# Order of the output products, of the output evictions and of one convolution eviction in a fused convolution, gate and projection kernel

## The chip, the cores and the metric

The kernel runs on one core of a Trainium2 chip. A core has a matrix engine (TensorE, PE in the profile; its weight loads are PEld), three engines for element-wise work (VectorE or DVE, ScalarE or ACT, GpSimd or POOL), a queue that only issues transfers here (SyncE or SP), and 16 DMA engines. Each engine works through its own instructions in the order in which they were written, and waits at an instruction until the others have reached what it needs. The metric is the device time of one execution in microseconds.

## The reference

The reference has two stages over x of 8 sequences, 4224 tokens and 192 channels, all in fp32.

```
w    = softmax(weight, axis=-1) # 8 heads x 7
y[s] = sum_k w[h, k] * x[s - 6 + k]  # per head of 24 channels
pre  = sum_k conv_w[k] * y[s - 4 + k]  # 5 taps per channel
gate = 1 / (1 + exp(-pre))
out  = (gate * (y @ w_val)) @ w_out # two 192 x 192 products
```

So each token takes a 7-tap convolution, a 5-tap gate with a sigmoid, a product with `w_val`, a multiplication by the gate, and a product with `w_out`.

## The kernel before, in words

The 192 channels lie on partitions as 128 plus 64. The token stream is cut in two streams, so that chunk 0 of a tile holds the first 128 channels of both streams side by side (128 x 2 x m), and chunk 1 the remaining 64 channels of one stream in partitions 0 to 63 and of the other in 64 to 127 (128 x m). A *block* is m tokens of each stream. There are 37 blocks, 0 to 36 (`N`, `LAST` = 36): two of 288, six of 432, 27 of 482, one of 500 and one of 244.

Per block the work is this.

- The 7-tap convolution is made on the matrix engine from overlapping windows of x, with the softmaxed taps as a band matrix (`conv_unit`, L303). A unit takes up to 7 windows of 8 small matmuls each (four 64-row pieces, each of two instructions) into two PSUM banks `pc`, and ScalarE copies each bank into a buffer `e` (the *evictions*, L330). From there DMAs scatter the rows into the tiles `x1` and `x2` (`scatter`, L359), and new windows are loaded (L165); both are issued by SP. The units of a group of blocks are made about two groups ahead. Blocks 5 to 28 take two units each, of 14, 13 and 13 windows in turn; block 29 takes two, blocks 30 and 31 one, later blocks none.
- The gate's taps: ScalarE makes the first tap into a PSUM tile (`gate_open`, L393: `pa` for chunk 0, `pb` for chunk 1), VectorE adds the four others (`gate_taps`, L400), ScalarE takes the sigmoid (`gate_close`, L413, which writes `g`). Each of `pa` and `pb` has one buffer, so a gate is opened only after the one before it was closed.
- The *value* product v = y @ w_val and the *output* product o of the block before it. Each has a third of its columns for chunk 1 (`v_2`, `o_2`: `diagonal` L456 and `columns` L490, plain fp32) and two thirds for chunk 0 of the two streams (`v_0`, `v_1`, `o_0`, `o_1`), which are made with operands split into a high and a low fp32r part: `rows` (L479, from chunk 1) and `main` (L466, from chunk 0), three products each.
- The high parts are casts on ScalarE (`xh`, `ph`, L421 for chunk 0 and L429 for chunk 1), the low parts subtractions on POOL (`xl`, `pl`, L422 and L430). `ph` and `pl` are those of the gated values, on which the output product works.
- VectorE multiplies the value product by the gate (`gated`, L508: g <- v, g), ScalarE copies the output product to `ot` (`project`, L524), and SP sends it out (L529).

All of this is written out by hand, engine by engine; nothing reorders it. The v, o and pc banks share one pool of five PSUM banks, `ps`, given out in turn. A block with two units takes ten, so each tile of a block gets the same bank every time: v_2 and o_1 the first, o_2 and the first unit's first pc the second, v_0 and its second pc the third, v_1 and the second unit's first pc the fourth, o_0 and the second unit's second pc the fifth. A matmul that writes a bank first waits until its last reader has finished.

From block 4 (`HEAD`) on the loop at the end of the kernel sets the order. In letters, A is a tap of chunk 0's gate and B one of chunk 1's. The two closings of a block are: first that of chunk 1 (after taps B A B A), later that of chunk 0 (after taps A B A B).

Of the kernel before, what the change touches and what calls it, by code (L numbers as in the profile page):

```python
# [33 lines left out]
NJS = [2, 3, 3, 3] + [5] * 9 + [3]  # L34
# [71 lines left out]
def kernel(  # L106
# [193 lines left out]
                units.append((g, q, ws[i : i + UNIT[n]]))  # L300
    first_unit = [next(i for i, u in enumerate(units) if u[0] == g) for g in range(NG)] + [len(units)]

    def conv_unit(u):  # L303
        g, q, ws = units[u]
        n = NJS[g]
        if u == first_unit[g]:
# [19 lines left out]
        a = ws[0][0] * n + ws[0][1]  # L326
        w = len(ws)
        ev = e[:, : 4 * n * WIN].rearrange("p (w r t) -> p w r t", r=2, t=HW)
        for r in range(2):
            nc.scalar.copy(ev[:, a : a + w, r, :], pc[r][:M, : w * HW].rearrange("p (w t) -> p w t", t=HW))  # L330
        done = [hi for hi, j in ws if j == n - 1]
        for hi in done:
            h = QUADS[q][hi]
# [71 lines left out]
    def gate_close(n, i):  # L405
        if n >= N:
            return
        m = STEPS[n][2]
        if i == 0:
            dst = g1s[n] = gp.tile([128, 2, MB], F32, tag="g1", name=f"g1_{n}")[:, :, :m]  # L410
        else:
            dst = g2s[n] = gp.tile([128, MB], F32, tag="g2", name=f"g2_{n}")[:, :m]
        nc.scalar.activation(dst, accs.pop((n, i)), AF.Sigmoid)  # L413
# [122 lines left out]
        at.append(at[-1] + m)  # L536
    done = [0]

    def conv(k):
        for _ in range(k):  # L540
            if done[0] < len(units):
                conv_unit(done[0])
                done[0] += 1

    todo = [0] * (N + 1)
# [69 lines left out]
    gate_taps(HEAD, 1)  # L615
    for i in range(2):
        gate_close(HEAD, i)
    for i in range(2):
        gate_open(HEAD + 1, i)

# [15 lines left out]
    def close():  # L636
        for n, i in pending:
            gate_close(n, i)
# [6 lines left out]
    for n in range(HEAD, N + 1):  # L645
        diagonal(n)
        taps({HEAD: "", HEAD + 1: "BBABA"}.get(n, "BABA"))
        close()
        if n <= LAST:
            split_gated1(n - 1)  # L650
        reopen()
        split(n + 1)
        columns("v", n)
        gated(n, 2)
        columns("o", n - 1)
        project(n - 1, 2)
        split_gated2(n)
        taps("AABAA" if n == HEAD else "ABAB")
        close()
        reopen()  # L660
        rows("v", n)
        rows("o", n - 1)
        main("v", n, 0)
        gated(n, 0)
        main("v", n, 1)
        gated(n, 1)
        if n == LAST:
            split_gated1(n)
        main("o", n - 1, 0)
        project(n - 1, 0)  # L670
        main("o", n - 1, 1)
        project(n - 1, 1)
        conv(todo[n])


# [75 lines left out]
```

## Time and profile before

| | |
|---|---|
| time before, median of 3 | 366.2 us (364.02, 366.20, 366.21) |
| the profiled execution | 368.63 us, its span 366.8 us |
| granted matrix clock, mean over the span | 0.98 (0.93 and 0.90 up to 80 us, then 1.00 up to 345 us) |
| time from a closing of chunk 0's gate to the next, blocks of 482 with two units | 9.21 to 9.26 us (one of 11.52, one of 9.96) |
| the same, blocks without units | 8.72 and 8.73 us |

The profiled execution is taken by the hardware profiler, and is 0.7% longer than the median. In the rows, the first number is the start in us from the start of the span, the second the length in us. Starts that lie closer together than the lengths are pipelined: what an instruction occupies of its engine is the distance to the next one's start. A bracket at the end of a row says how long the engine was idle before it, and what ended this.

### The profile page before, as it was taken

What the parts mean: (1) busy time and instruction counts of PE and PEld (TensorE: products, weight loads), DVE (VectorE), ACT (ScalarE), POOL (GpSimd) and SP (SyncE); (2) the same over time, 40 slices, a digit from 0 to 9 for tenths busy, and PEclk for the clock granted to TensorE, in tenths of its full rate; (3) what the DMA queues carried; (4) which work ended last, traced back from release to release, by engine and by line L of the source; (5) the groups of instructions that cost most, each with busy time, mean ns of one, the idle gap of its engine ahead of it and who ended that gap; (6) DMA issues with size and microseconds to landing.
All of it is one profiled execution on the core that took longest, in us unless ns stands there. A gap on an engine that the chain in (4) does not pass through costs nothing.

```text
span 366.8 us, 13015 instructions
## 1 busy us (share of the span) xinstructions
PE 340.6 (93%) x5316; PEld 220.7 (60%) x5316; DVE 326.2 (89%) x439; ACT 306.4 (84%) x538; POOL 266.8 (73%) x209
## 2 busy tenths in 40 slices
PE   8887889799988999999999999999999999999995
PEld 8766456566655666665666666566666666554453
DVE  4898498989997999999999999899999999999970
ACT  7588588799886889889889889889889888888773
POOL 1959534677777777777777777777777777888883
PEclk9899699899999999999999999999999999999999
DMA  8899779898995998998998798898799796432233
GB/s 278 241 230 264 226 220 287 211 264 269 210 291 163 213 281 266 206 283 269 206 289 267 203 287 266 202 281 272 183 288 283 188 270 201 143 117 83 81 158 132
DMA packets 38948, 83.20 MB, mean 227 GB/s; under 512 B 4936, under 2 KB 17008, under 8 KB 38888
## 3 DMA queue, kind: packets, MB, share of 16 engines
q1 hardware_dynamic: 37440, 80.64, 74.6%
q0 software_dynamic: 896, 1.27, 1.5%
q8 instruction: 42, 0.69, 0.8%
q10 hardware_dynamic: 552, 0.46, 0.4%
q14 instruction: 18, 0.15, 0.2%
HBM read 30.06 MB, written 26.00 MB: 153 GB/s over the span
## 4 chain that ended last, share of the span: by engine, by line
PE 32%; DVE 30%; ACT 19%; DMA 9%; issue 6%; SPq 3%; DVEq 0%; POOL 0%; ACTq 0%
DVE pa L400 19%; PE pc L319 9%; PE v L490 7%; ACT pa L393 7%; ACT g L413 7%; DMA x<-xw 7%; DVE pb L400 7%; PE o L456 5%; DVE g L508 5%; ACT ot L524 4%; PE v L456 3%; PE v L466 2%; PE o L466 2%; DMA x<-e 2%; SPq L359 1%
## 5 line engine op out<-in xcount | busy, mean ns | idle before, releaser
L400 DVE SCALAR_TENSOR_TENSOR pa<-x,cwt,pa 128x964 f32<-128x964 f32 (+4 forms) x148 | 173.3, 1171 | 0.8 <-ACT pa L393 0.4
L422 POOL TENSOR_TENSOR pl<-g,ph 128x964 fp32r<-128x964 f32 (+4 forms) x37 | 80.0, 2161 | 75.6 <-ACT ph L421 70.1
L400 DVE SCALAR_TENSOR_TENSOR pb<-x,cwt,pb 128x482 f32<-128x482 f32 (+4 forms) x148 | 102.9, 695 | 0.6
L508 DVE TENSOR_TENSOR g<-v,g 128x482 f32<-128x482 f32 (+4 forms) x111 | 66.6, 630 | 25.8 <-PE v L490 21.0
L319 PE MATMUL pc<-band,x 64*64 64x58 f32 (+1 forms) x3776 | 75.3, 222 | 13.8 <-ACT ot L524 7.4
L319 PEld LDWEIGHTS pc<-band,x 64*56 64x56 f32 (+1 forms) x3776 | 66.3, 134 | 28.5 <-ACT ot L524 11.0
L422 POOL TENSOR_TENSOR xl<-x,xh 128x964 fp32r<-128x964 f32 (+4 forms) x37 | 73.4, 1984 | 3.3 <-ACT xh L421 3.3
L330 ACT COPY e<-pc 120x348 f32<-120x348 f32 (+2 forms) x148 | 59.3, 485 | 4.0 <-PE pc L319 3.9
L524 ACT COPY ot<-o 128x482 f32<-128x482 f32 (+4 forms) x111 | 57.2, 547 | 5.3 <-PE o L466 2.9
L413 ACT ACTIVATE g<-pa 128x964 f32<-128x964 f32 (+4 forms) x37 | 34.8, 940 | 30.8 <-DVE pa L400 30.8
L430 POOL TENSOR_TENSOR xl<-x,xh 128x482 fp32r<-128x482 f32 (+4 forms) x37 | 42.0, 1135 | 6.4 <-ACT xh L429 3.8
L430 POOL TENSOR_TENSOR pl<-g,ph 128x482 fp32r<-128x482 f32 (+4 forms) x37 | 43.2, 1167 | 1.5 <-ACT ph L429 1.5
L393 ACT ACTIVATE pa<-x,cwt 128x964 f32<-128x964 f32 (+4 forms) x37 | 38.1, 1030 | 1.9 <-DMA x<-e 0.7
L490 PE MATMUL v<-x,wvf 128*64 128x482 f32 (+4 forms) x148 | 37.3, 583 | 2.3 <-issue 2.3
L456 PE MATMUL o<-g,wof 64*64 64x482 f32 (+4 forms) x148 | 37.8, 572 | 0.2 <-issue 0.2
L421 ACT CAST ph<-g 128x964 fp32r<-128x964 f32 (+4 forms) x37 | 36.3, 980 | 1.8 <-POOL pl L430 1.8
L456 PE MATMUL v<-x,wvf 64*64 64x482 f32 (+4 forms) x148 | 36.5, 561 | 0.0
L421 ACT CAST xh<-x 128x964 fp32r<-128x964 f32 (+4 forms) x37 | 36.2, 979 | 0.0
L490 PE MATMUL o<-g,wof 128*64 128x482 f32 (+4 forms) x148 | 35.0, 550 | 0.0
L466 PE MATMUL v<-xh,wvh 128*128 128x482 f32 (+4 forms) x74 | 31.7, 429 | 0.0
L466 PE MATMUL o<-pl,woh 128*128 128x482 f32 (+4 forms) x74 | 27.5, 371 | 1.0 <-POOL pl L422 1.0
L466 PE MATMUL v<-xh,wvl 128*128 128x482 f32 (+4 forms) x74 | 27.8, 375 | 0.0
(68 smaller groups left out, 481.3 us busy)
## 6 DMA issues: line engine op xcount, KB each, us to landing
x<-xw SPq DMA_DIRECT2D x72, 300.0 KB
out<-ot SPq DMA_DIRECT2D x27, 723.0 KB
x<-e SPq DMA_DIRECT2D x45, 271.9 KB
x<-xw SPq DMA_DIRECT2D x16, 360.0 KB
x<-e SPq DMA_DIRECT2D x36, 135.9 KB
out<-ot SPq DMA_DIRECT2D x6, 648.0 KB
x<-e SPq DMA_DIRECT2D x20, 163.1 KB
x<-e SPq DMA_DIRECT2D x18, 90.6 KB
```

The lines of the kernel that those rows point to most:

```text
L319: nc.tensor.matmul(pc[r][c0:c1, k * HW : (k + 1) * HW], lhsT=xtiles[i][p, c + c0 : c + c1], rhs=band[p, 4 * q + hi, :], start=True, stop=True,
L393: nc.scalar.mul(acc, views(n, 0)[i], cwt[:, i, 0:1])
L400: nc.vector.scalar_tensor_tensor(out=acc, in0=views(n, k)[i], scalar=cwt[:, i, k : k + 1], in1=acc, op0=ALU.mult, op1=ALU.add,)
L413: nc.scalar.activation(dst, accs.pop((n, i)), AF.Sigmoid)
L421: nc.scalar.copy(h, x)
L422: nc.gpsimd.tensor_tensor(out=l, in0=x, in1=h.bitcast(F32), op=ALU.subtract)
L430: nc.gpsimd.tensor_tensor(out=l, in0=x, in1=h.bitcast(F32), op=ALU.subtract)
L456: nc.tensor.matmul(dst, lhsT=w22, rhs=x[HALVES[r]], start=True, stop=False)
L466: nc.tensor.matmul(acc, lhsT=a[:, r], rhs=b[:, q], start=(fresh and i == 0), stop=(not fresh and i == 2))
L490: nc.tensor.matmul(acc[HALVES[q if what == "v" else 1 - q]], lhsT=w.f[:, W12 : W12 + 64], rhs=x[:, q], start=False, stop=True)
L508: nc.vector.tensor_tensor(out=v, in0=banks.pop(("v", n, q)), in1=v, op=ALU.mult)
L524: nc.scalar.copy(ots[n][:, q * m : (q + 1) * m], banks.pop(("o", n, q)))
```

## The change

From block 4 on, five things stand in another order. No instruction is added or taken away, and the order on VectorE, POOL and SP is the same as before.

1. In blocks 4 to 35 the output product's `rows` and `main` go ahead of the value product's `main`, `rows` of o also ahead of `rows` of v. Since banks are given out in turn, the banks move too: o_0 takes the third bank, o_1 the fourth, v_0 the fifth and v_1 the first, which is that of v_2 of the same block.
2. With them `project` moves: ScalarE copies o_0 and o_1 to `ot` ahead of the second closing (chunk 0's gate), and not behind the opening that follows it.
3. The cast `ph` of the block before (`split_gated1`) goes ahead of the first closing (chunk 1's gate), and not behind it.
4. The second eviction of a block's last unit, and the scatters and loads that stand behind it, are held back until the first closing of the next block has been issued (`hold`, `held`, `release`).
5. In block 4 the cast of block 3 goes ahead of the two openings of the gates of block 5; blocks 36 and 37 keep the old order of the products.

```
-        for r in range(2):
+        def evict(r):
             nc.scalar.copy(ev[:, a : a + w, r, :], pc[r][:M, : w * HW]...)
+        evict(0)
+        if hold:
+            held.append(lambda: (evict(1), send_rows(g, q, ws, e)))
+        else:
+            evict(1)
+            send_rows(g, q, ws, e)
...
     for i in range(2):
         gate_close(HEAD, i)
+    split_gated1(HEAD - 1)
     for i in range(2):
         gate_open(HEAD + 1, i)
...
         diagonal(n)
         taps({HEAD: "", HEAD + 1: "BBABA"}.get(n, "BABA"))
+        if HEAD < n <= LAST:
+            split_gated1(n - 1)
         close()
-        if n <= LAST:
-            split_gated1(n - 1)
+        release()
         reopen()
...
+        def outputs():
+            for q in range(2):
+                main("o", n - 1, q)
+                project(n - 1, q)
+
+        if n < LAST:
+            rows("o", n - 1)
+            rows("v", n)
+            outputs()
+        else:
+            rows("v", n)
+            rows("o", n - 1)
         close()
         reopen()
-        rows("v", n)
-        rows("o", n - 1)
-        main("v", n, 0)
-        gated(n, 0)
-        main("v", n, 1)
-        gated(n, 1)
+        for q in range(2):
+            main("v", n, q)
+            gated(n, q)
         if n == LAST:
             split_gated1(n)
-        main("o", n - 1, 0)
-        project(n - 1, 0)
-        main("o", n - 1, 1)
-        project(n - 1, 1)
-        conv(todo[n])
+        if n >= LAST:
+            outputs()
+        conv(todo[n], True)
```

ScalarE before, from the closing of chunk 0's gate of block 12 (in the loop's block 11) to that of block 13; the first number in a name is the block, or the unit for pc:

```order
L413 ACTIVATE g1_12_2271<-pa_12_2126 128x2x482
L393 ACTIVATE pa_13_2273<-x1_5_1406,cwt_155 128x2x482
L524 COPY ot_10_2261<-o_10_0_2283 128x482
L524 COPY ot_10_2261<-o_10_1_2284 128x482
L330 COPY e_7_0_2310<-pc_34_0_2311 120x7x58
L330 COPY e_7_0_2310<-pc_34_1_2312 120x7x58
L330 COPY e_7_0_2310<-pc_35_0_2347 120x7x58
L330 COPY e_7_0_2310<-pc_35_1_2348 120x7x58
L413 ACTIVATE g2_12_2393<-pb_12_2246 128x482
L421 CAST ph_11_2395<-g1_11_2124 128x2x482
L393 ACTIVATE pb_13_2399<-x2_5_1407,cwt_155 128x482
L421 CAST xh_13_2405<-x1_5_1406 128x2x482
```

ScalarE after, at the same place, from the copies of o_10 on:

```order
L542 COPY ot_10_2261<-o_10_0_2271 128x482
L542 COPY ot_10_2261<-o_10_1_2272 128x482
L431 ACTIVATE g1_12_2296<-pa_12_2151 128x2x482
L411 ACTIVATE pa_13_2298<-x1_5_1406,cwt_155 128x2x482
L331 COPY e_7_0_2310<-pc_34_0_2311 120x7x58
L331 COPY e_7_0_2310<-pc_34_1_2312 120x7x58
L331 COPY e_7_0_2310<-pc_35_0_2347 120x7x58
L439 CAST ph_11_2388<-g1_11_2149 128x2x482
L431 ACTIVATE g2_12_2392<-pb_12_2246 128x482
L331 COPY e_7_0_2310<-pc_35_1_2348 120x7x58
L411 ACTIVATE pb_13_2399<-x2_5_1407,cwt_155 128x482
L439 CAST xh_13_2405<-x1_5_1406 128x2x482
```

The two copies to ot moved over the closing and the opening, the cast ph moved over one closing and one eviction, and that eviction moved behind the closing.

The matrix engine before, `rows` of block 12's values and of block 11's outputs, with what each waits for:

```order
L479 MATMUL v_12_0_2428<-xh2_12_2248,wvh_157 128x482 [waits Activation_49,Pool_49]
L479 MATMUL v_12_1_2429<-xh2_12_2248,wvh_157 128x482 [waits Activation_49]
L479 MATMUL v_12_0_2428<-xh2_12_2248,wvl_158 128x482
L479 MATMUL v_12_1_2429<-xh2_12_2248,wvl_158 128x482
L479 MATMUL v_12_0_2428<-xl2_12_2249,wvh_157 128x482 [waits Pool_49]
L479 MATMUL v_12_1_2429<-xl2_12_2249,wvh_157 128x482
L479 MATMUL o_11_0_2436<-ph2_11_2263,woh_161 128x482 [waits Activation_49]
L479 MATMUL o_11_1_2437<-ph2_11_2263,woh_161 128x482 [waits DVE_49]
```

The matrix engine after, at the same place:

```order
L497 MATMUL o_11_0_2424<-ph2_11_2263,woh_161 128x482 [waits Activation_49]
L497 MATMUL o_11_1_2425<-ph2_11_2263,woh_161 128x482 [waits Activation_49]
L497 MATMUL o_11_0_2424<-ph2_11_2263,wol_162 128x482
L497 MATMUL o_11_1_2425<-ph2_11_2263,wol_162 128x482
L497 MATMUL o_11_0_2424<-pl2_11_2264,woh_161 128x482 [waits Pool_49]
L497 MATMUL o_11_1_2425<-pl2_11_2264,woh_161 128x482
L497 MATMUL v_12_0_2432<-xh2_12_2248,wvh_157 128x482 [waits Activation_49]
L497 MATMUL v_12_1_2433<-xh2_12_2248,wvh_157 128x482 [waits DVE_49]
```

The wait for VectorE, which is for the multiplication that frees v_2's bank, stood on o_1 as the second of these pairs, and stands on v_1 now, again in the second half.

The matrix engine before, `main` of the same block:

```order
L466 MATMUL v_12_0_2428<-xh_12_2252,wvh_157 128x482
L466 MATMUL v_12_0_2428<-xh_12_2252,wvl_158 128x482
L466 MATMUL v_12_0_2428<-xl_12_2253,wvh_157 128x482
L466 MATMUL v_12_1_2429<-xh_12_2252,wvh_157 128x482
L466 MATMUL v_12_1_2429<-xh_12_2252,wvl_158 128x482
L466 MATMUL v_12_1_2429<-xl_12_2253,wvh_157 128x482
L466 MATMUL o_11_0_2436<-ph_11_2395,woh_161 128x482 [waits Activation_49]
L466 MATMUL o_11_0_2436<-ph_11_2395,wol_162 128x482
L466 MATMUL o_11_0_2436<-pl_11_2396,woh_161 128x482 [waits Pool_49]
```

The matrix engine after, at the same place:

```order
L484 MATMUL o_11_0_2424<-ph_11_2388,woh_161 128x482
L484 MATMUL o_11_0_2424<-ph_11_2388,wol_162 128x482
L484 MATMUL o_11_0_2424<-pl_11_2389,woh_161 128x482 [waits Pool_49]
L484 MATMUL o_11_1_2425<-ph_11_2388,woh_161 128x482
L484 MATMUL o_11_1_2425<-ph_11_2388,wol_162 128x482
L484 MATMUL o_11_1_2425<-pl_11_2389,woh_161 128x482
L484 MATMUL v_12_0_2432<-xh_12_2252,wvh_157 128x482
L484 MATMUL v_12_0_2432<-xh_12_2252,wvl_158 128x482
L484 MATMUL v_12_0_2432<-xl_12_2253,wvh_157 128x482
```

The product of pl_11 with o_0 stood ninth of the twelve, and stands third now; the values stand six matmuls later.

More of the change, by code (lines that the diff above doesn't have):

```diff
@@ L301, with conv_unit @@
     first_unit = [next(i for i, u in enumerate(units) if u[0] == g) for g in range(NG)] + [len(units)]
-    def conv_unit(u):
+    def conv_unit(u, hold=False):
         g, q, ws = units[u]
@@ L328, in conv_unit, with release, send_rows @@
         ev = e[:, : 4 * n * WIN].rearrange("p (w r t) -> p w r t", r=2, t=HW)
-        for r in range(2):
+        def evict(r):
             nc.scalar.copy(ev[:, a : a + w, r, :], pc[r][:M, : w * HW].rearrange("p (w t) -> p w t", t=HW))
+        evict(0)
[4 more added lines that the diff above has]
+            send_rows(g, q, ws, e)
+    held = []
+    def release():
+        for f in held:
+            f()
+        held.clear()
+    def send_rows(g, q, ws, e):
+        n = NJS[g]
         done = [hi for hi, j in ws if j == n - 1]
@@ L537, with conv @@
     done = [0]
-    def conv(k):
-        for _ in range(k):
+    def conv(k, hold=False):
+        for i in range(k):
             if done[0] < len(units):
-                conv_unit(done[0])
+                conv_unit(done[0], hold and i == k - 1)
                 done[0] += 1
@@ L658 @@
         taps("AABAA" if n == HEAD else "ABAB")
+        def outputs():
[9 more added lines that the diff above has]
+            rows("o", n - 1)
         close()
         reopen()
-        rows("v", n)
-        rows("o", n - 1)
-        main("v", n, 0)
-        gated(n, 0)
-        main("v", n, 1)
-        gated(n, 1)
+        for q in range(2):
+            main("v", n, q)
+            gated(n, q)
         if n == LAST:
             split_gated1(n)
-        main("o", n - 1, 0)
-        project(n - 1, 0)
-        main("o", n - 1, 1)
-        project(n - 1, 1)
-        conv(todo[n])
+        if n >= LAST:
+            outputs()
+        conv(todo[n], True)
+    assert not held
 def kernel(x, weight, moe_w_val, moe_conv_w, moe_w_out):
```

## The prediction

> **What bounds the kernel now.** I read the page's busy shares first, then the busy times block by block, then the chain of waits through one block, then the waits. The busy shares alone do not decide; the table by block does more. It shows three blocks of 482 with two units, one of those with a stop, and two late blocks without a second unit. Its columns are the stretch and its length, the busy time of PE, PEld, DVE, ACT and POOL, the granted clock, the DMA share and GB/s.
>
> ```profile
> PE 340.6 (93%) x5316; PEld 220.7 (60%) x5316; DVE 326.2 (89%) x439; ACT 306.4 (84%) x538; POOL 266.8 (73%) x209
> ```
>
> ```profile
> 134.32:143.58 9.26, 9.05 (x154) 5.80 (x153) 8.82 (x12) 8.39 (x14) 6.95 (x6) 1.00 0.94 290
> 143.58:152.81 9.23, 8.89 (x146) 5.61 (x145) 8.83 (x12) 8.29 (x14) 7.32 (x6) 1.00 0.80 203
> 152.81:162.07 9.26, 9.04 (x146) 5.74 (x145) 8.82 (x12) 8.29 (x15) 7.28 (x6) 1.00 0.98 271
> 226.80:236.76 9.96, 9.42 (x146) 5.64 (x145) 8.82 (x12) 8.29 (x14) 8.08 (x6) 1.00 0.81 198
> 319.42:328.15 8.73, 8.73 (x90) 4.96 (x89) 8.73 (x12) 7.59 (x13) 7.25 (x6) 1.00 0.34 123
> ```
>
> No engine fills the 9.25 us of a block: VectorE is busy for 8.82, ScalarE for 8.3 to 8.4, POOL for 7. In the last row VectorE has the same twelve instructions and no idle time, and a block takes 8.73. So 0.5 us of a normal block is waiting that VectorE's work does not need. The chain of waits for the block from 134.32 (start, length, what) shows where it is lost.
>
> ```profile
> 134.32 0.99 ACT g L413
> ...
> 135.34 1.07 ACT pa L393
> 136.41 0.50 ACT ot L524
> ...
> 136.95 0.98 PE pc L319 x49
> ...
> 138.83 0.98 PE v L490 x4
> ...
> 139.94 0.66 DVE g L508
> 140.60 1.14 DVE pa L400
> 141.73 0.63 DVE pb L400
> 142.36 1.14 DVE pa L400
> ...
> 143.58 0.99 ACT g L413
> ```
>
> This is a closed loop. The closing of chunk 0's gate (L413), the opening behind it, 2.09 us together, then the copy of o_0 to ot, 0.54 with its hand-over, which frees the bank for the second unit; 1.88 of convolution and diagonals, 1.11 of columns, then VectorE's multiplication and three taps, 3.64, up to the next closing. The sum is 9.26, the block's own time; nothing else has to be slow for the block to take that long. Its marks are these waits (window 100 to 300: in total, times, longest).
>
> ```profile
> ACT g L413 <- DVE pa L400: 20.5, 21, 1.9
> DVE g L508 <- PE v L490: 12.2, 22, 2.7
> PE pc L319 <- ACT ot L524: 5.2, 20, 0.4
> ```
>
> **The change.** *The copies to ot ahead of the closing* cut this loop. The copy of o_0 no longer stands behind two ScalarE instructions that wait for VectorE, so the second unit has its bank in time. The copies themselves cost the same. What a block takes then is the longest of four things.
>
> VectorE: 8.73, from the late block. ScalarE and POOL are shorter. The matrix engine's own time is the block less the gap in which it issues nothing. For the gaps:
>
> ```profile
> 135.61 1.14 PE L319 MATMUL pc<-band,x 64*64 64x58 f32 x58
> 136.95 0.98 PE L319 MATMUL pc<-band,x 64*56 64x58 f32 x53 [0.21 <-ACT ot L524]
> 137.77 0.22 PE L319 MATMUL pc<-band,x 64*64 64x58 f32 x1
> 144.85 1.02 PE L319 MATMUL pc<-band,x 64*64 64x58 f32 x50
> 146.21 0.97 PE L319 MATMUL pc<-band,x 64*56 64x58 f32 x53 [0.34 <-ACT ot L524]
> ```
>
> One such matmul is 0.22 from issue to end, so the last before the stop was issued at 135.61 + 1.14 - 0.22 = 136.53, and the next at 136.95: 0.42 lost. In the next block it is 146.21 - 145.65 = 0.56. The floors are 9.26 - 0.42 = 8.84 (14 windows) and 9.23 - 0.56 = 8.67 (13 windows), 8.73 on average over the three blocks of a group.
>
> The busy column would give another answer: 9.05, 8.89 and 9.04, mean 8.99, and so a saving of only 0.25 a block. The last row of the table speaks against it, since there the matrix engine is "busy" for all 8.73 us with 90 recorded matmuls in place of 146 to 154. The Trainium skill, Perfetto Trace Analysis, section Identifying the Most-Contended Engine, says that matmul busy time is no good measure of headroom because matmuls are pipelined; the trace agrees, by those 90. By the busy column the sum below would be 5.5 us from blocks 8 to 29, by the issue gaps it is 8.7.
>
> *Outputs ahead of values* makes two loops that need prices. I use these rows, the last three of them from a late block in which half a pair of rows waited for the multiplication:
>
> ```profile
> 136.34 1.01 ACT L524 COPY ot<-o 128x482 f32<-128x482 f32 x2
> 137.24 1.70 ACT L330 COPY e<-pc 120x406 f32<-120x406 f32 x4
> 138.80 0.62 ACT L413 ACTIVATE g<-pb 128x482 f32<-128x482 f32 x1
> 139.26 1.04 ACT L421 CAST ph<-g 128x964 fp32r<-128x964 f32 x1
> 140.38 2.27 POOL L422 TENSOR_TENSOR pl<-g,ph 128x964 fp32r<-128x964 f32 x1 [2.23 <-ACT ph L421]
> 143.44 0.38 PE L466 MATMUL o<-ph,woh 128*128 128x482 f32 x1
> 144.02 1.22 DVE L508 TENSOR_TENSOR g<-v,g 128x482 f32<-128x482 f32 x2
> 144.53 0.38 PE L466 MATMUL o<-pl,woh 128*128 128x482 f32 x1
> 333.23 0.66 DVE L508 TENSOR_TENSOR g<-v,g 128x482 f32<-128x482 f32 x1
> 333.94 0.49 PE L479 MATMUL o<-ph,woh 64*128 64x482 f32 x1 [0.78 <-DVE g L508]
> 334.80 0.49 PE L466 MATMUL v<-xh,wvh 128*128 128x482 f32 x1
> ```
>
> First loop: the multiplication of chunk 1 frees the bank of v_1's rows (0.71 from its start), then 0.86 to the first main product, 1.47 for the six of o (143.44 to 144.91), 0.04 and 0.45 for the second copy to ot (half of 136.34 to 137.24), 1.02 for the closing, 1.12 for the opening with its hand-over, and three taps, 2.90, to the next multiplication: 8.57. It is no bound. Second loop: closing 1.02, opening 1.00, three evictions 1.17 (three quarters of 137.24 to 138.80), cast to subtraction 1.12, subtraction 2.27, hand-over 0.05, from the third product to the end of o_1 1.03, copy 0.49, next closing: 8.15. No bound either, with 0.6 us to spare against 8.73.
>
> *The cast ahead of the first closing, and the eviction behind it*, are what keeps that second loop short: in the old order a closing (0.46) and an eviction (0.39) would lie in it, and it would be 9.00. Against that stand two delays. The closing of chunk 1 comes at 1.02 + 1.00 + 1.17 + 0.88 = 4.07 us behind that of chunk 0 (before: 138.80 - 134.32 = 4.48), so it is not later at all. The held eviction starts at 4.07 + 0.46 = 4.53, where the last one ended at about 4.5 before; its bank is wanted by v_0's rows only after 5.2 (the multiplication's start in the loop, 139.94 - 134.32 = 5.62, less the 0.4 by which a block shortens), when o's columns and rows still have to run. SP's next scatters and loads leave 0.4 us later; their order on SP is the old one, and what they feed is wanted blocks later. I cost these at nothing. Without cover the eviction would cost 0.43 a block, by its own length.
>
> VectorE's two multiplications of chunk 0 get their inputs six matmuls later, 1.3 us (six spacings of 0.22). Before, v_0 was complete at 142.94 (four spacings ahead of 143.44, and 0.38), 1.08 ahead of VectorE's 144.02, so 0.24 us a block is exposed for as long as the matrix engine is not further ahead; its floor lets it run ahead. I allow for this: the four floors (8.73, 8.73, 8.57, 8.15) lie so close that I take the longest single one, the 8.84 of a block with 14 windows, rounded to 8.85, and keep 8.73 and 9.0 as ends.
>
> **The sum.** The blocks and the other places:
>
> ```profile
> 104.33 0.98 ACT L413 ACTIVATE g<-pa 128x964 f32<-128x964 f32 x1 [0.98 <-DVE pa L400]
> 310.70 0.98 ACT L413 ACTIVATE g<-pa 128x964 f32<-128x964 f32 x1 [0.98 <-DVE pa L400]
> 111.04 1.03 PE L490 MATMUL v<-x,wvf 128*64 128x482 f32 x4 [2.27 <-issue]
> 74.50 0.61 DVE L508 TENSOR_TENSOR g<-v,g 128x432 f32<-128x432 f32 x1 [1.91 <-PE v L490]
> 83.04 0.61 DVE L508 TENSOR_TENSOR g<-v,g 128x432 f32<-128x432 f32 x1 [0.49 <-PE v L490]
> ```
>
> From 104.33 to 310.70 are 22 blocks, 206.37 us. Two stops in it, 2.27 at 111.04 and 0.71 (9.96 less 9.25), have no releaser that the change touches, and stay. The rest is 203.4, 9.245 a block. At 8.85 the saving is 22 x 0.395 = 8.7 us (11.3 at 8.73, 5.4 at 9.0). Blocks 5 to 7, still partly of 432 tokens, lose 0.49 or less on VectorE; I take 0.33 each, 1.0. Between blocks 4 and 5 it loses 1.91; there the cast now stands ahead of two openings and delays VectorE by about 0.8, and I take 0.8 net, between 0 and 1.9. Blocks 31 to 34 run at VectorE's pace already: nothing. In block 35 the values come 1.3 us later in a kernel that is running out of other work; before, the last output product waited for POOL anyway, so I cost it at 0.2 of loss (0 to 1.3). Together 10.3 us. The profiled execution of 368.63 us (366.8 of it span) would come to 358.3. It lies 0.7% above the median of 366.2, so the time is 358.3 x 366.2 / 368.63 = 356.0.
>
> **The rivals.** *The bubble only moves* (0.12). There are still five banks for ten tiles, and v_1's rows now wait where o_1's did. If the matrix engine's gap of 0.42 to 0.56 reappears there, the loop through it sets the same time: with all of it 366, with half of it a block of 9.0 and 360. For it: this wait is real in the late blocks, 0.78 above. Against: the loop behind it is 8.57. The Trainium skill, Perfetto Trace Analysis, section Identifying Performance Opportunities, says that the same gap repeating on an engine can mean too little PSUM for the next tile. By that rule an order alone moves the gap, and the time is this rival's; the trace shows that the present gap is a bank's, but also that the bank is late because of the two instructions ahead of its copy.
>
> *POOL's subtraction becomes the bound* (0.09, slower). The third product of o_0 needs pl, six matmuls earlier than now. If the cast could start no sooner behind the closing than before (139.26 - 134.32 = 4.94, because the evictions ahead of it wait for the convolution), the second loop would be 4.94 + 1.12 + 2.27 + 0.05 + 1.03 + 0.49 = 9.90, 0.65 a block more than now. It decides from a start at 4.29 on. Half way, 4.62, gives 9.58 a block: 22 x 0.33 = 7.3 us more, about 373. For it: POOL waits 2.23 for this cast now. Against: on paper the cast starts at 3.2.
>
> *The DMA engines become the bound* (0.09). Two blocks in three show shares of 0.94 and 0.98. If the latter is a limit, that block cannot go below 0.98 x 9.26 = 9.07, and the mean is (9.07 + 8.85 + 8.85) / 3 = 8.92: 1.6 us less saved, 357.6. Against: the bytes do not follow the share, 290 GB/s at 0.94 and 271 at 0.98, and loads may spill into the third block.
>
> *The change has no such effect*, because the copies, though ahead, end at the same moment (0.02): 366.
>
> **How the numbers follow.** The forecast has 0.68. The range goes from 8.73 a block with 1.9 in block 4 (11.3 + 1.5 + 1.9 = 14.7 less on 368.63, 351.6 as a median) to the first rival: I set 352 to 363.5, which leaves out the slow rival and most of the first. Below 362.5 (faster by over 1%, about what can be told apart) lie the forecast, the DMA case and a quarter of the first rival: 0.80. Within 1%: the rest of the first and the last, 0.11. Slower: 0.09.
>
> **What would show it.** In the profile after, a block of 482 takes 8.75 to 8.95, not 9.25; the wait of pc for ot is gone; the multiplication of chunk 1 waits less than 0.2 for its columns; the closing of chunk 0 waits less than 0.5 for VectorE. A wait of v's rows for VectorE's multiplication, repeating, shows the first rival; one of o's main product for pl shows POOL's; a block time that goes up and down with the DMA share shows the third. The forecast is wrong if a block stays above 9.0.

## The result, and the profile after

| | before | after |
|---|---|---|
| median of the runs | 366.2 us (364.02 to 367.37) | 354.49 us (352.68 to 356.59) |
| ratio, 95% interval | 1 | 0.969 (0.961 to 0.976) |
| the profiled execution, its span | 368.63 us, 366.8 us | 356.59 us, 354.8 us |
| a block of 482 tokens with two units | 9.21 to 9.26 us (one of 11.52, one of 9.96) | 8.81 to 8.89 us (one of 9.22) |

The kernel after is 3.1% faster; 356.0 us were predicted.

The busy times of the page of after, and then, from the chain that ended last, the shares by engine, of before and of after:

```profile
PE 334.3 (94%) x5316; PEld 216.6 (61%) x5316; DVE 327.1 (92%) x439; ACT 309.9 (87%) x538; POOL 267.0 (75%) x209
```

```profile
PE 32%; DVE 30%; ACT 19%; DMA 9%; issue 6%; SPq 3%; DVEq 0%; POOL 0%; ACTq 0%
```

```profile
PE 68%; DVE 12%; DMA 7%; ACT 4%; issue 4%; POOL 4%; SPq 1%; DVEq 0%; POOLq 0%; ACTq 0%
```

Busy times have hardly moved, as they must when no instruction is added. The chain has: before, it went around through ScalarE, the matrix engine and VectorE, and after, it is mostly a string of matmuls. The table by block shows three blocks in a row (columns as in the prediction: stretch and length, busy PE, PEld, DVE, ACT, POOL, clock, DMA share, GB/s).

```profile
120.02:128.89 8.87, 8.87 (x145) 5.63 (x144) 8.87 (x12) 8.39 (x16) 7.25 (x6) 1.00 0.96 289
128.89:137.76 8.87, 8.87 (x153) 5.72 (x152) 8.87 (x12) 8.49 (x15) 6.99 (x6) 1.00 0.91 293
137.76:146.58 8.82, 8.82 (x145) 5.63 (x144) 8.82 (x12) 8.40 (x15) 7.28 (x6) 1.00 0.83 228
```

Both the matrix engine and VectorE now count as busy for all of a block. The waits (window 100 to 300: in total, times, longest) show what has gone. The three waits that the prediction quoted of before, pc for ot, the closing for VectorE's tap and the multiplication of chunk 1 for its columns, no longer appear. Beside waits of weight loads (PEld), which overlap with matmuls, what is left is POOL, which may wait, and these two:

```profile
ACT ot L542 <- PE o L484: 7.4, 23, 0.6
...
DVE g L526 <- PE v L484: 0.2, 1, 0.2
```

The whole run divides so, by the closings of chunk 0's gate. The last column is a second execution of the same kernel, told of below as `e14_after_again`.

| stretch | before | after | after, second profile |
|---|---|---|---|
| start to the closing ahead of block 4 (not touched by the change) | 60.35 | 59.10 | 57.36 |
| from there to the closing in block 8 (the prediction's blocks 4 to 7) | 43.98 | 42.89 | 44.17 |
| the 22 blocks that follow (its blocks 8 to 29) | 206.37 | 195.20 | 194.91 |
| last stretch, to the end | 56.10 | 57.61 | 55.96 |
| span | 366.8 | 354.8 | 352.4 |

Only the third row moves by more than executions of one kernel differ among themselves. It gave 11.2 and 11.5 us. Of this, 2.98 us are the two stops of the profile before (2.27 and 0.71), where the first profile after has one of 0.35 and the second none. Without stops the 22 blocks took 203.4 and 194.9 us, so the shorter block itself is worth 8.5 us.

### The profile page after: what moved, and what is told of

Same layout as the page of the kernel before. It is cut to its first block, busy times and chain, and to the rows that moved or that the text cites. A ratio compares the mean times of both kernels' runs of the same rounds, so it can differ in the third digit from the quotient of the medians.

```text
span 354.8 us, 12959 instructions
## 1 busy us (share of the span) xinstructions
PE 334.3 (94%) x5316; PEld 216.6 (61%) x5316; DVE 327.1 (92%) x439; ACT 309.9 (87%) x538; POOL 267.0 (75%) x209
## 4 chain that ended last, share of the span: by engine, by line
PE 68%; DVE 12%; DMA 7%; ACT 4%; issue 4%; POOL 4%; SPq 1%; DVEq 0%; POOLq 0%; ACTq 0%
PE pc L319 13%; PE o L484 12%; PE v L484 10%; PE v L508 7%; DVE pa L418 6%; PE o L497 6%; PE o L508 6%; PE v L497 5%; DMA x<-xw 5%; PE v L474 4%; PE o L474 4%; DVE pb L418 3%; DVE g L526 2%; PE pw L208 2%; ACT g L431 2%
## 5 line engine op out<-in xcount | busy, mean ns | idle before, releaser
L319 PE MATMUL pc<-band,x 64*64 64x58 f32 (+1 forms) x3776 | 66.4, 221 | 9.8 <-DMA x<-xw 4.7
L542 ACT COPY ot<-o 128x482 f32<-128x482 f32 (+4 forms) x111 | 60.4, 548 | 16.3 <-PE o L484 12.6
L319 PEld LDWEIGHTS pc<-band,x 64*56 64x56 f32 (+1 forms) x3776 | 60.9, 133 | 21.4 <-issue 12.9
L331 ACT COPY e<-pc 120x348 f32<-120x348 f32 (+2 forms) x148 | 61.4, 472 | 3.2 <-PE pc L319 3.2
L474 PE MATMUL v<-x,wvf 64*64 64x482 f32 (+4 forms) x148 | 38.2, 563 | 0.0
L484 PE MATMUL o<-ph,woh 128*128 128x482 f32 (+4 forms) x74 | 31.5, 425 | 0.0
L484 PE MATMUL o<-pl,woh 128*128 128x482 f32 (+4 forms) x74 | 27.9, 377 | 0.7 <-POOL pl L440 0.7
L484 PE MATMUL v<-xh,wvh 128*128 128x482 f32 (+4 forms) x74 | 28.1, 380 | 0.0
```

Of the source, the lines that this page charges most:

```text
L319: nc.tensor.matmul(pc[r][c0:c1, k * HW : (k + 1) * HW], lhsT=xtiles[i][p, c + c0 : c + c1], rhs=band[p, 4 * q + hi, :], start=True, stop=True,
L474: nc.tensor.matmul(dst, lhsT=w22, rhs=x[HALVES[r]], start=True, stop=False)
L484: nc.tensor.matmul(acc, lhsT=a[:, r], rhs=b[:, q], start=(fresh and i == 0), stop=(not fresh and i == 2))
L542: nc.scalar.copy(ots[n][:, q * m : (q + 1) * m], banks.pop(("o", n, q)))
```

## The experiments

All times are set against the kernel before, run on the same chip; "block" is the time from one closing of chunk 0's gate to the next in the middle of the kernel.

| run | what it changes in the kernel after | median us | ratio to before (95%) | block us |
|---|---|---|---|---|
| `e1_copies_behind` | copies to ot behind closing and opening | 380.1 | 1.040 (1.034 to 1.045) | 9.33, 9.93, 9.98 |
| `e2_cast_and_hold` | products and copies in the old order | 366.2 | 1.004 (1.001 to 1.008) | 9.23 to 9.33 |
| `e3_outputs_only` | cast in the old place, nothing held | 374.2 | 1.024 (1.019 to 1.029) | 9.50 |
| `e5_cast_behind` | cast in the old place | 376.2 | 1.030 (1.024 to 1.036) | 9.50 |
| `e4_no_hold` | nothing held | 354.2 | 0.969 (0.965 to 0.974) | 8.82 to 8.89 |
| `e14_after_again` | nothing | 353.4 | 0.968 (0.963 to 0.973) | 8.81 to 8.89 |
| `e6_pe_light` | four matmuls of a block left out | 352.8 | 0.963 (0.958 to 0.969) | 8.73 |
| `e7_dve_light` | one tap of a block left out | 355.1 | 0.971 (0.967 to 0.976) | 8.82 to 8.89 |
| `e8_vrows_late` | rows of v behind the main products of o | 359.1 | 0.981 (0.975 to 0.988) | 8.97 to 9.15, mean 9.07 |
| `e13_switches` | rows of v in two pieces between them | 369.6 | 1.012 (1.006 to 1.018) | 9.40 to 9.53 (two of 11.1 with a stop) |
| `e15_swap` | closing ahead of the second copy, taps A A B B | 359.7 | 0.983 (0.979 to 0.987) | 8.99 |
| `e10_head` | cast of block 3 behind the two openings | 354.4 | 0.970 (0.965 to 0.975) | 8.81 to 8.88 |

### Which part of the change brings it

`e1_copies_behind` keeps the products' new order and puts the copies back behind the closing:

```
             rows("v", n)
-            outputs()
+            for q in range(2):
+                main("o", n - 1, q)
...
         reopen()
+        if n < LAST:
+            for q in range(2):
+                project(n - 1, q)
```

> The products in the order of the kernel after, but both copies to ot back behind the closing and the opening of chunk 0's gate. Theory (the place of the copies sets the loop): the banks that they free are now those of the first unit's second pc and of the second unit's first, so all of the convolution stands behind them: closing and opening 2.09, copy 0.54, from the first convolution matmul to the last columns 2.77 + 1.1 (129.64 to 132.41 and the columns, in the trace after), VectorE's multiplication and three taps 3.64, together 10.1 a block in place of 8.87, so 22 x 1.25 = 27 us more than the kernel after, about 382; pc waits for ot in each block. Rival (the gain comes from the products' order and from where the cast and the eviction stand, the copies being hidden): about 355, a block of 8.85 to 8.9.

Measured: 380.1 us, 4% slower than before. Its waits (window 110 to 290: in total, times, longest) name the cause:

```profile
PE pc L319 <- ACT ot L542: 13.0, 13, 1.1
```

So it is the copies' place, and the new order of the products without it is worse than the old one. The size was overrated: 9.75 a block on average and not 10.1.

`e2_cast_and_hold` keeps only the cast ahead of the first closing and the held eviction:

```
-        if n < LAST:
+        if n < HEAD:
             rows("o", n - 1)
...
-        if n >= LAST:
+        if n >= HEAD:
             outputs()
```

> Only ScalarE's two smaller moves (the cast ahead of the first closing, the held eviction); products and copies in the order of before. Theory (the loop through the copies is left as it was): a block of 9.2 to 9.3 and a time of 366, within 2 us of before; pc waits for ot 0.2 to 0.4 in each block. Rival (the cast was what was late, and the copies only went along with it): a block below 9.0 and a time of 355 to 358.

Measured: 366.2 us, 0.4% above before, blocks of 9.23 to 9.33. ScalarE's two smaller moves alone bring nothing; the loop through the copies stands as the prediction had it.

`e3_outputs_only` does the reverse: products and copies are moved, the cast and the eviction are not.

```
-        if HEAD < n <= LAST:
-            split_gated1(n - 1)
         close()
+        if HEAD < n <= LAST:
+            split_gated1(n - 1)
         release()
...
-        conv(todo[n], True)
+        conv(todo[n])
```

> Only the products' order and the copies; the cast stands behind the first closing and no eviction is held. The prediction's own price for the second loop without the two moves: 9.00 a block, 22 x 0.13 = 3 us more than the kernel after, about 357.5. A second reading of the same loop: the first closing (chunk 1) ends when VectorE's taps do, 4.1 after the closing of chunk 0 in the trace after (128.89 to 132.97), so the cast would start at 4.55, and 4.55 + 1.12 + 2.27 + 0.05 + 1.03 + 0.49 = 9.5: 22 x 0.63 = 14 us more, about 368, slower than before, with the third product of o_0 waiting for POOL. Rival (the cast has slack, 0.8 in the trace after, and more is hidden): 354.5 to 355.5.

Measured: 374.2 us, 2.4% slower than before. Every block takes 9.50, as the second reading had it, and not 9.00. One block of its timeline, from the closing of chunk 0 (ScalarE, then POOL, then the matrix engine; the bracket is the idle time ahead, and what ended it):

```profile
139.57 0.98 ACT L431 ACTIVATE g<-pa 128x964 f32<-128x964 f32 x1
...
143.58 0.57 ACT L431 ACTIVATE g<-pb 128x482 f32<-128x482 f32 x1 [0.40 <-DVE pb L418]
144.05 0.99 ACT L439 CAST ph<-g 128x964 fp32r<-128x964 f32 x1
```

```profile
145.11 2.27 POOL L440 TENSOR_TENSOR pl<-g,ph 128x964 fp32r<-128x964 f32 x1 [2.16 <-ACT ph L439]
```

```profile
147.44 0.49 PE L484 MATMUL o<-pl,woh 128*128 128x482 f32 x1 [0.40 <-POOL pl L440]
```

The closing of chunk 1 waits 0.40 for VectorE's last tap, the cast starts 144.05 - 139.57 = 4.48 behind the closing of chunk 0, and the third product of o_0 waits for pl. With that start the prediction's formula for POOL's rival gives 4.48 + 1.12 + 2.27 + 0.05 + 1.03 + 0.49 = 9.44. The slower rival was thus a true mechanism, and it is the cast's move alone that keeps the kernel out of it. That the held eviction has no part in it is shown by the two runs that follow.

`e5_cast_behind` moves the cast alone back (the first piece of the diff of `e3_outputs_only`).

> The kernel after, but with the cast behind the first closing again; the eviction stays held. By the prediction's own sum for the second loop (ScalarE's instructions one behind the other): 8.15 + 0.46 = 8.61, below the 8.87 of now, so no change, 354.5. By the reading with which the run of the products' order alone agreed (the first closing ends when VectorE's taps of chunk 1 do, 4.1 behind the closing of chunk 0, and the cast starts at 4.55): 9.5 a block and 373 to 375, as in that run, where the eviction was not held.

Measured: 376.2 us, and 9.50 a block.

`e4_no_hold` drops the held eviction alone (the second piece of that diff).

> The kernel after, but without the held eviction: both evictions of the last unit stand ahead of the cast. Theory (0.8 us of slack at the third product of o_0, of which an eviction takes 0.39): a block of 8.85 to 8.9, the time within 1 us of 354.5. Rival (the last eviction waits for the convolution and holds up the cast, as behind the closing in the old order): 0.4 to 0.6 a block more, 363 to 368.

Measured: 354.2 us, the time of the kernel after. The held eviction neither costs nor brings anything.

`e10_head` puts the cast of block 3 behind the two openings again:

```
-    split_gated1(HEAD - 1)
     for i in range(2):
         gate_open(HEAD + 1, i)
+    split_gated1(HEAD - 1)
```

> The kernel after, but in block 4 the cast of block 3 stands behind the two openings again, as in the kernel before. By the prediction: block 4 takes 7.4 in place of 8.2 (VectorE waited 1.01 for the opening), while the main products of the outputs wait for pl some 1.9 longer than the 0.73 of now and the next block starts later by 0.8 to 1.1: net within 0.5 us of the kernel after. Rival (the delay of the cast is hidden by the convolution that follows): 0.8 us less, 353.7. Other rival (the delay comes through in full): 1.1 us more, 355.6.

Measured: 354.4 us, no difference that can be told. Block 4 takes 7.58 in place of 8.20, and the main products of o wait for pl 1.50 in place of 0.73. What the next block makes of it can't be read, since the granted clock in it differs from one execution to the next (last section).

### What a block is bound by now

The prediction took the matrix engine's 8.84. Two kernels that leave work out ask which engine it is.

`e6_pe_light`:

```
         for i, (a, b) in enumerate(parts(w, h2, l2)):
+            if n > HEAD and i == 1:
+                continue
             for acc, p in zip(two, HALVES):
```

> The kernel after, but from block 5 on the second of the three products of the rows (low part of the weight by the high part of chunk 1) is left out, for values and for outputs: four matmuls in two pairs, 0.22 us a pair, 0.43 a block of the matrix engine's time. If the matrix engine alone sets the 8.87 of a block, VectorE's floor of 8.73 comes next: 0.14 a block over some 26 blocks, 3 to 4 us less than the kernel after, about 351. If VectorE alone sets it: no change, 354.5. If a loop through the products to the closing sets it, which gets shorter by the 0.43 too: below 8.6 a block, 347 or less.

`e7_dve_light`:

```
             if n < N:
-                gate_taps(n, i, k, k + 1)
+                if not (i == 1 and k == 2):
+                    gate_taps(n, i, k, k + 1)
                 at_tap[i] += 1
```

> The kernel after, but from block 5 on one of the four taps of chunk 1 is left out on VectorE: 0.65 us a block. If the matrix engine sets the 8.87 of a block: no change, 8.85 to 8.9 and 354 to 355. If its floor is the 8.73 worked out from issue gaps and VectorE adds the rest: 8.73, about 351. If VectorE sets it: 8.87 less 0.65 = 8.2 a block, 337 to 340.

Measured: 352.8 and 355.1 us. The intervals of the two ratios overlap with each other and with that of the kernel after, so the time of a block has to decide. Two blocks of each, first without the matmuls, then without the tap:

```profile
142.97:151.69 8.72, 8.72 (x141) 5.33 (x140) 8.72 (x12) 8.49 (x14) 7.17 (x6) 1.00 0.95 296
151.69:160.42 8.73, 8.73 (x150) 5.46 (x148) 8.73 (x12) 8.50 (x14) 6.99 (x6) 1.00 0.91 276
```

```profile
139.29:148.13 8.84, 8.84 (x145) 5.63 (x144) 8.29 (x10) 8.40 (x15) 7.32 (x6) 1.00 0.89 252
148.13:157.01 8.88, 8.88 (x146) 5.61 (x144) 8.29 (x10) 8.40 (x16) 7.25 (x6) 1.00 0.98 289
```

With less work on the matrix engine the block falls to VectorE's 8.73, and to the same 8.73 with 13 windows as with 14. With less work on VectorE nothing changes. So VectorE's 8.73 is the next floor, and what sets 8.86 goes through the products. Is it the matrix engine's own time? That was asked by moving the rows of v out of the way.

`e8_vrows_late`:

```
             rows("o", n - 1)
-            rows("v", n)
             outputs()
+            rows("v", n)
```

> The kernel after, but with the rows of the values behind the main products of the outputs and not ahead of them, in all blocks up to 35. That takes the first loop (v_1's bank, which VectorE's multiplication frees) out of the way of the copies and the closing, and it asks for pl 0.65 us earlier, of the 0.8 that it has to spare. By the prediction's loops: no bound moves, 8.87 a block, 354 to 354.5, of that up to 0.5 less in the blocks without units, where v_1's rows wait 0.3 to 1.2 now. If the first loop does set part of the 8.87: a block of 8.75 and 351.5. If pl has less to spare than the trace seems to show: the third product of o_0 waits for POOL, and a block takes up to 0.5 more, 360 and above.

Measured: 359.1 us and 9.07 a block, 0.21 more. The size would fit the third reading, but no wait for pl, or any other of the matrix engine, is shown for it. Its timeline shows what it is. The matrix engine of the kernel after, from the columns of one block to its next convolution (L497 are the rows, L484 the main products):

```profile
131.24 0.58 PE L474 MATMUL v<-x,wvf 64*64 64x482 f32 x1
...
131.46 0.62 PE L474 MATMUL o<-g,wof 64*64 64x482 f32 x2
...
132.41 1.03 PE L508 MATMUL v<-x,wvf 128*64 128x482 f32 x4
...
134.18 0.48 PE L497 MATMUL o<-ph,woh 64*128 64x482 f32 x2
...
135.69 0.49 PE L484 MATMUL o<-ph,woh 128*128 128x482 f32 x1
...
138.50 1.68 PE L319 MATMUL pc<-band,x 64*64 64x58 f32 x102
```

The same of `e8_vrows_late`:

```profile
140.63 0.58 PE L474 MATMUL v<-x,wvf 64*64 64x482 f32 x1
140.64 0.61 PE L474 MATMUL o<-g,wof 64*64 64x482 f32 x1
...
141.64 1.03 PE L508 MATMUL v<-x,wvf 128*64 128x482 f32 x4
...
143.40 0.49 PE L497 MATMUL o<-ph,woh 64*128 64x482 f32 x2
143.73 0.38 PE L497 MATMUL o<-ph,wol 64*128 64x482 f32 x2
143.95 0.39 PE L497 MATMUL o<-pl,woh 64*128 64x482 f32 x2
144.27 0.49 PE L484 MATMUL o<-ph,woh 128*128 128x482 f32 x1
...
148.16 1.68 PE L319 MATMUL pc<-band,x 64*64 64x58 f32 x102
```

Two things differ. The rows and main products take 148.16 - 143.40 = 4.76 here and 138.50 - 134.18 = 4.32 there, for the same 24 matmuls: there are four groups of one kind in place of two, and at a change of kind the spacing is 0.32 or 0.33, not 0.22. Two more groups cost 0.44. And the diagonals are *shorter*: 141.64 - 140.63 = 1.01 here, 132.41 - 131.24 = 1.17 there (1.26 and 1.29 in the two blocks that follow). Where o_2's diagonal is issued 0.01 behind v_2's here (0.17 and 0.05 in the two blocks that follow), it comes 0.22 to 0.34 behind it there. In the kernel after, something holds it, although the list of the matrix engine's waits is empty.

`e13_switches` has still more changes of kind (`rows` now takes as a third argument which of its three products it makes):

```
             rows("o", n - 1)
-            rows("v", n)
-            outputs()
+            main("o", n - 1, 0)
+            project(n - 1, 0)
+            rows("v", n, (0,))
+            main("o", n - 1, 1)
+            project(n - 1, 1)
+            rows("v", n, (1, 2))
```

> The kernel after, but the rows of the values are cut in two and put between the main products of the outputs: rows of o, main of o_0, the first rows product of v, main of o_1, the other two rows products of v, main of v. The same matmuls, with four more changes between 64-row products (rows) and 128-row products (main) than in the kernel after. Theory (each change costs the matrix engine 0.10 us: in the run with the rows of v behind the outputs, a product that follows another kind starts 0.32 behind it and not 0.22, two more changes made 0.20 of a block, and no wait is shown): 4 x 0.10 = 0.4, a block of 9.25 to 9.3 and about 363 to 364. Rival (what cost 0.2 there was that pl is wanted earlier, or that VectorE then waited up to 0.3 for v_0): pl is wanted no earlier than there and the values come no later, so 9.07 again, 359, or less.

Measured: 369.6 us and a block of 9.40 to 9.53. The rival is out; the theory had the size wrong.

```profile
157.31 0.48 PE L499 MATMUL o<-ph,woh 64*128 64x482 f32 x2
...
158.16 0.49 PE L484 MATMUL o<-ph,woh 128*128 128x482 f32 x1
...
159.02 0.48 PE L499 MATMUL v<-xh,wvh 64*128 64x482 f32 x2
159.43 0.49 PE L484 MATMUL o<-ph,woh 128*128 128x482 f32 x1
...
```

One pair of rows alone between two main products takes 159.43 - 159.02 = 0.41 and not 0.22, and each group of three 0.85 or 0.86 and not 0.65: a group costs 0.20 beside its matmuls. Four more groups are 0.8, less some 0.2 that the diagonals give back as in the run before; 0.61 was measured. The Trainium skill, TensorEngine Tiling (Array Packing), section Key Properties, says that changing the tiling mode drains the matrix engine. The traces agree that a change costs time, 0.20 us a group here; that a drain is the reason, no run shows. By this price, the matrix engine alone would need at most 9.07 - 0.44 = 8.63 for a block of the kernel after. That is an estimate from the two timelines, and it is less than 8.86.

What then holds o_2's diagonal? By the order of the banks it takes the one of the first unit's first pc, so it waits until ScalarE has made the block's first eviction. ScalarE of after, in the two blocks from 128.89:

```profile
128.89 0.98 ACT L431 ACTIVATE g<-pa 128x964 f32<-128x964 f32 x1
...
130.91 1.28 ACT L331 COPY e<-pc 120x406 f32<-120x406 f32 x3
...
137.76 0.98 ACT L431 ACTIVATE g<-pa 128x964 f32<-128x964 f32 x1
...
139.78 1.19 ACT L331 COPY e<-pc 120x348 f32<-120x348 f32 x3
```

The matrix engine, in the second of them:

```profile
139.98 0.58 PE L474 MATMUL v<-x,wvf 64*64 64x482 f32 x1
...
140.28 0.62 PE L474 MATMUL o<-g,wof 64*64 64x482 f32 x2
```

The diagonal starts 0.55 behind the start of an eviction of 406 columns (131.46 - 130.91) and 0.50 behind one of 348 (140.28 - 139.78). From it to the next closing it is 6.30 both times (137.76 - 131.46 and 146.58 - 140.28). So there is a third loop: closing and opening 2.02, first eviction 0.50 or 0.55, o_2's diagonal to the end of o_1 and its copy 6.30. The prediction had not listed it. That its sum is 8.82 or 8.87 proves nothing by itself, since every chain from one closing to the next adds up to a block. Two things speak for it.

First, a block's length follows its first eviction and not its windows. In the table by block, the blocks from 120.02 and from 137.76 have 13 windows each, and that from 128.89 has 14 (eight more matmuls, 0.12 us). Yet the block from 120.02 takes 8.87 like the one of 14, and only the block from 137.76 takes 8.82. The first eviction of the former is of 406 columns, as in the block of 14; it is the second unit that has a window less. If the matrix engine's own time set the block, the two of 13 windows would be alike. So it goes on: every third block is the shorter one.

```profile
122.04 1.24 ACT L331 COPY e<-pc 120x406 f32<-120x406 f32 x3
```

Second, in `e6_pe_light` the weight load of o_2's diagonal is shown to wait for ScalarE's eviction in every block (window 130 to 290: in total, times, longest). In the block from 142.97 the eviction starts at 144.98 and the diagonal at 145.53, again 0.55 later.

```profile
PEld o L474 <- ACT e L331: 5.2, 18, 0.4
```

`e15_swap` was to cut this loop, by taking the second copy out of it:

```
-        taps("AABAA" if n == HEAD else "ABAB")
+        taps("AABAA" if n == HEAD else "AABB")
...
-            outputs()
+            main("o", n - 1, 0)
+            project(n - 1, 0)
+            main("o", n - 1, 1)
+            close()
+            project(n - 1, 1)
         else:
             rows("v", n)
             rows("o", n - 1)
-        close()
+            close()
```

> The kernel after, with two more moves in blocks 5 to 35: the closing of chunk 0's gate goes ahead of the copy of o_1 to ot (the opening stays behind the copy), and VectorE makes chunk 0's last two taps one behind the other (A A B B in place of A B A B), so that this closing can come 0.63 earlier against its other work. Theory (a third loop sets the 8.87 of a block: closing and opening 2.02, the block's first eviction 0.49, which frees the bank that o_2's diagonal wants, from that diagonal to the end of o_1 5.81, from 131.46 to 137.27 in the trace after, the second copy to ot 0.49, together 8.8 to 8.85): the copy and the matrix engine's part leave the loop, VectorE's 8.73 is next, 0.13 a block over some 25 blocks, 3 us less than the kernel after, 350.5 to 351.5. Rival (the matrix engine's own time sets the 8.87): no change, 354. Other rival (the matrix engine, whose convolution then starts some 0.7 later against the closing, delivers v_0 too late for VectorE): a block of 9.0 or more, 357.

Measured: 359.7 us and 8.99 a block, also in the late blocks without a second unit. The last reading had the size, but not the reason: no wait of VectorE for v_0 is shown. VectorE's rows tell why:

```profile
142.88 1.22 DVE L418 SCALAR_TENSOR_TENSOR pa<-x,cwt,pa 128x964 f32<-128x964 f32 x1
144.01 0.65 DVE L526 TENSOR_TENSOR g<-v,g 128x482 f32<-128x482 f32 x1
144.58 2.48 DVE L418 SCALAR_TENSOR_TENSOR pa<-x,cwt,pa 128x964 f32<-128x964 f32 x2
146.97 1.48 DVE L418 SCALAR_TENSOR_TENSOR pb<-x,cwt,pb 128x482 f32<-128x482 f32 x2
148.36 1.22 DVE L526 TENSOR_TENSOR g<-v,g 128x482 f32<-128x482 f32 x2
```

Two taps of chunk 0 one behind the other occupy 146.97 - 144.58 = 2.39, where one with another instruction behind it occupies 1.13 (144.01 - 142.88): 0.13 more for the pair. The two taps of chunk 1 take 1.39, against twice 0.63 where they stand alone: 0.13 again. 8.73 + 0.26 = 8.99. The edit brought VectorE a cost of its own, which hid what the loop may have given. The third loop is therefore shown by its times in the traces, by the wait in `e6_pe_light` and by the runs with less work on either engine, but not by its removal. No version here that does all of the work is faster than the kernel after; `e4_no_hold` does the same with less code.

### The last blocks

The profile given with the result had a last stretch of 57.61 us, 1.5 longer than before. `e14_after_again` is the unchanged kernel.

> The kernel after, unchanged, for a second profiled execution. Theory (the 1.4 us by which the blocks without units were longer than in the run without the held eviction, 44.39 against 42.99, come from the granted clock, 0.85 over one block of that one execution, and not from the order): in an execution whose clock stays at 1.00 there, the five blocks before the last closing take 43.0 and the rest is as it was. Rival (the wait of 1.19 us in front of v_1's rows lowers the clock each time): 44.4 again, with a clock below 0.9 in the third of these blocks.

Measured: 353.4 us, and the five blocks take 42.98. The clock was the difference; more of it in the last section.

## Why the prediction was right

**The loop of before.** Right: with the copies in their old place the time is that of before (`e2_cast_and_hold`) or worse (`e1_copies_behind`), and pc's wait for ot comes back with them (in the first, 0.4 at most, 21 times between 100 and 300 us).

**8.85 a block, 22 x 0.395 = 8.7 us.** Right in size: 195.20 / 22 = 8.87 with one stop of 0.35 in it, 8.86 in the second profile. The reason was only half right. Of the four floors, VectorE's 8.73 is exact (`e6_pe_light`). The matrix engine's 8.84 and 8.67, from issue gaps, were not what binds: its own time is at most about 8.63, and the loop through the first eviction and o_2's bank, which was not on the list, gives 8.82 and 8.87. That 8.84 came out so near to 8.86 was luck. "I take the longest single one" was a choice that allowed for couplings not yet seen, and one such was there.

**The cast ahead of the closing.** Right in kind, too small: "it would be 9.00" without the cast and the held eviction; 9.50 was measured. The step that failed is the sum of ScalarE's own instructions. The closing ahead of the cast doesn't follow them; it waits 0.40 for VectorE's tap. With the start of 4.48 from the trace, the prediction's own rival gives 9.44. The change has the cast in its new place, so this error didn't reach the time.

**The held eviction at nothing; the values 1.3 us later, 0.24 a block exposed.** The first is shown by `e4_no_hold`. Of the second nothing is left in the long run: one wait of 0.2 in the window.

**The two stops, 2.98 us, "stay".** They did not: 0.35 in the same place after, none in the second profile. So they differ from one execution to another; how often the kernel before has them is open, since there is one profile of it. They stood in the sum on the profiled execution, where the scaling to the median covered a part of them.

**Blocks 4 to 7, 1.8 us.** 1.09 in one profile, a loss of 0.19 in the other, so no gain is shown and none is ruled out. The step that failed is to read VectorE's wait of 1.91 between blocks 4 and 5 as one of order. The stretch in which it stands had a low clock:

```profile
67.75:77.84 10.09, 9.11 (x193) 6.77 (x194) 8.14 (x12) 8.70 (x17) 5.87 (x6) 0.83 0.89 249
```

At that clock the same stretch of after takes 10.41 (below), and VectorE's wait in it is 1.78; at full clock it takes 8.95, and the wait is 0.36.

**The end, 0.2 us of loss.** Right to about 0.3 us: 55.96 against 56.10 where the clock is at 1.00 in the late blocks, and the wait for v_0 in block 35 that was foreseen is there (1.26).

**The sum.** 10.2 us between the medians were predicted, and 11.7 measured. The blocks gave 8.5 of the 8.7. The 1.8 of blocks 4 to 7 is not seen. What the other 3.2 are stays open: the stretch that the change doesn't touch alone differs by up to 3.0 between the profiles. That the total came this close is in part luck.

**The rivals.** DMA is out: a block takes 8.87 at a share of 0.96 in the kernel after, and 8.72 at 0.95 with fewer matmuls (`e6_pe_light`). That the bubble only moves was wrong for three quarters of it. The Trainium skill, Perfetto Trace Analysis, section Identifying Performance Opportunities, reads a gap that repeats as a possible lack of PSUM. Here an order alone took 0.39 of the 0.52 by which a block stood above VectorE's 8.73, and the 0.13 that remains hangs on a bank again, that of o_2. POOL as the bound was a true mechanism, which the cast's move avoids.

## What to carry to other kernels

When a block lasts longer than any engine is busy, look for the loop that closes through a buffer: who frees it, and what stands ahead of the freeing instruction on its engine. Moving the copies ahead of two instructions, of which the first waits for another engine, gave 3%, with no instruction less; but the same move makes an operand wanted earlier, and without its cast moved too it would have cost 2 to 3%. After such a cut, write down the loops through *every* buffer in the new order: the one that set the new time was one that nobody had listed, and in this kernel it showed as a late issue and not as a wait.

## What the runs showed of the hardware

**The clock falls in one execution and not in another, at the same waits.** Block 5 and the first of the late blocks without units, in the kernel after, first and second profile:

```profile
67.30:76.25 8.95, 7.60 (x140) 5.27 (x141) 8.55 (x12) 8.59 (x17) 4.82 (x5) 1.00 0.88 257
...
314.56:324.36 9.80, 8.61 (x40) 4.89 (x39) 9.26 (x12) 7.09 (x11) 8.47 (x7) 0.85 0.19 77
```

```profile
65.56:75.97 10.41, 9.05 (x140) 5.92 (x141) 8.60 (x12) 8.79 (x17) 5.85 (x5) 0.84 0.89 248
...
313.81:322.53 8.72, 7.54 (x42) 4.04 (x41) 8.72 (x12) 7.11 (x11) 7.40 (x6) 1.00 0.21 87
```

The clock falls in block 5 in the second profile and in the late block in the first, and the block is longer by 1.5 and 1.1 us. The waits of the matrix engine in them are the same in both profiles: 1.02 and 0.88 against 1.00 and 0.88 in block 5, and one of 1.19 against one of 1.18 in the late block.

```profile
320.35 0.48 PE L497 MATMUL v<-xh,wvh 64*128 64x482 f32 x1 [1.19 <-DVE g L526]
```

```profile
319.60 0.48 PE L497 MATMUL v<-xh,wvh 64*128 64x482 f32 x1 [1.18 <-DVE g L526]
```

The mean over a block hides what the clock does. In shorter stretches of the late block, first profile:

```profile
320.00:321.00 1.00, 0.65 (x5) 0.48 (x5) 1.00 (x2) 1.00 (x2) 0.92 (x2) 1.00 0.00 0
321.00:322.00 1.00, 1.00 (x5) 0.72 (x3) 1.00 (x3) 0.79 (x2) 1.00 (x2) 0.68 0.08 16
322.00:324.00 2.00, 2.00 (x6) 1.66 (x5) 1.82 (x3) 0.66 (x2) 2.00 (x2) 0.50 0.00 0
324.00:325.00 1.00, 1.00 (x4) 0.82 (x4) 0.00 (x0) 1.00 (x2) 0.93 (x1) 0.61 0.00 0
```

It is at 1.00, then at 0.50 for 0.64 + 2.00 + 0.78 = 3.42 us, then at 1.00 again, and the main products in it start 0.40 apart and not 0.22. In block 5 of the second profile it is at 0.50 for 3.4 us too. The Trainium skill, TensorE: Matmul & The Clock Gate, section What's actually happening, says that the clock is either full or half, by how busy the engine was in windows of about 3.4 us that run on their own and do not start with the kernel. The traces agree with the two values and with the length. The section ties the half clock to an idle window, while no single wait here is over 1.2 us; why the clock fell in one execution and not in the other, no run shows. So a gain of 1 us read from a stage with such waits needs more than one profile.

**A change between rows and main products costs the matrix engine 0.20 us a group**, as told above, and **two taps in a row on the same accumulator cost VectorE 0.13 us more than two with another instruction between**.
